# Weight combinations by groups of 128 columns, and three weights decoded in the second part without ScalarE functions

## The chip, the cores and the metric

The kernel runs on one core of a Trainium2 chip. The metric is the time of one execution on the device in microseconds. The engines are named as in the profile: PE (TensorE matmuls), PEld (TensorE weight loads), DVE (VectorE), ACT (ScalarE), POOL (GpSimd), SP (SyncE, which here issues every DMA).

## What is computed

Three layers follow one another on 4 x 3072 tokens of width 256. The float64 weights of the second and third layer arrive as pairs of 32-bit words.

```python
def _attn_ref(x, w_r, w_i, b_r, b_i):              # layer 1: FFT, complex mixing, soft threshold
    X = np.fft.rfft(x, axis=1); Xr, Xi = X.real, X.imag
    Yr = Xr @ w_r - Xi @ w_i + b_r
    Yi = Xr @ w_i + Xi @ w_r + b_i
    Y = soft(Yr, 0.01) + 1j * soft(Yi, 0.01)
    return np.fft.irfft(Y, n=x.shape[1], axis=1)
def _moe_ref(x, w_in, w_out):                      # layer 2: 256 -> 2048 -> 256
    h = x @ w_in
    return (h * np.tanh(softplus(h))) @ w_out
def _moe2_ref(x, mu_k, mu_r, w_k, w_v, w_r):       # layer 3: 256 -> 1024 -> 256, gated
    xk = mu_k * x + (1 - mu_k) * x_prev;  xr = mu_r * x + (1 - mu_r) * x_prev
    k = np.maximum(xk @ w_k, 0)
    return sigmoid(xr @ w_r) * (k * k @ w_v)
```

## The kernel before

**Two parts.** `part1` (L649) does the FFT layer. It runs 48 steps `u`, 12 for each of the four batches. A step emits a forward product F(u+1) (8 matmuls), the mixing product M(u) (13) and the inverse product I(u-1) (8), with the ScalarE and VectorE work that reads their banks: `post_F` (copy `xh`, remainder `xl`), `post_M` and `post_M2` (soft threshold `yb`), `post_I` (copy `bs`, then its store to `b_dr`). Butterflies of the FFT fill DVE in the background: `Background` (L415) keeps a clock of its own, and `bg.until` emits background operations until that clock has reached a time; where a step has weight work to do, 2100 ns are put on that clock (L864, L880). The engines work in the order in which the program emits.

**Float32 by two halves.** A matmul operand is held as a high part (`fp32r`) and a low part (what is left), so that one product is three matmuls: high x high, high x low, low x high.

**Seven products in place of eight.** The first product of layers 2 and 3 multiplies 2 x 2 blocks by seven block products. The four weight blocks and four sums of them are eight fields, of which seven are kept as high and low parts, 14 x 128 columns for each group. `MOVING` (L626) says which combination of the tokens meets which of the seven.

**Decoding the weights.** `raw_piece` (L499) loads 256 x 256 float64 values as words. `decode` (L505) makes float32 of them in stages: on ACT `sg` = sign (Copy with a scale, then Sign) and later Abs of the number; on DVE a xor and shift of the high word, an or with the shifted low word, and `min` times `sg`; then ACT copies the high part and DVE subtracts it. `pair_pieces` (L560) decodes two pieces, makes the four sums over 256 columns, splits and stores two groups. `Weights` (L593) is the pipeline: each `vec()` takes a new piece and advances the three before it, `sca` does the ACT stages and then issues the next loads. In steps 6 to 14 (`PARK_AT`, L41) `w_k` goes through it, 4 pieces, stored to `k_dr`. In the 12 steps of the last batch 8 pieces of `w_in` (stored to `h_dr`) and 8 of `w_out` (kept in SBUF) go through it, two pieces a step (L874 to L880). The first loads are issued in step 35.

**Part 2 by a planner.** `part2` (L909) hands every operation to `Plan` (L97) with an engine, a holding time and a due time. The plan runs the list in modelled time: an engine that is free takes the ready operation with the least due time, however far off that due time is, and this order is what is emitted. There are 12 stretches `J` of 1024 tokens, each 8 groups `n` of layer 2 (planned 10.22 us each, `at(n)`), then 48 groups of layer 3. A group (`group`, L934) is seven products into banks `x`, `c`, `d`, `z` with ACT copies between them (`c<-x`, `d<-x`, `zs<-z`) and two DVE sums (`k<-c`, `k<-d`); `outs_of` (L988) then makes the function of the result (ACT Mish in layer 2), its high and low parts (`h`, `l`) and the second product (`a<-h,wo`). `moving` (L1056) makes the combinations of the tokens, in the order of `MOVING`. `f3_job` (L1083) does the rest of the FFT butterflies on DVE. Weights `wr` of layer 2 are loaded again for each group from `h_dr`.

**The five pieces decoded in part 2** (L1156 to L1187): `w_v` (4 pieces) and the gate's weight, one after the other through one tile `dec`, each with a load, two ACT operations for the sign (`a1` Copy, `a2` Sign), `v1`, `v2` on DVE, `a3` Abs on ACT, `v3` on DVE, `a4` and `v4` for the two parts, and a store. They start behind the last butterfly job, with due times from `at(64)` on and 40 us apart. `dec_done`, the last store, is what the loads of layer 3's weights (`wk`, `wv`, L1212) and of the gate's operand (L1266) wait for.

Of the kernel before, what the change touches and what calls it, by code (L numbers as in the profile page):

```python
# [11 lines left out]
F32 = mybir.dt.float32  # L12
F32R = mybir.dt.float32r
I32 = mybir.dt.int32
# [26 lines left out]
PARK_AT = (6, 15)  # L41
# [127 lines left out]
def tile_fft_mix_moe_channel_mix(  # L169
# [26 lines left out]
    def emit(ops):  # L196
        for e in ops:
            e()

    def tt(o, a, b, op):  # L200
        V.tensor_tensor(out=o, in0=a, in1=b, op=op)  # L201
# [4 lines left out]
    def act(o, i, f, **kw):  # L206
        S.activation(out=o, in_=i, func=f, **kw)  # L207
# [291 lines left out]
    def raw_piece(src):  # L499
        raw = pools["st"].tile([128, 512, 2], I32, tag="raw", name="raw", bufs=4)  # L500
        nc.sync.dma_start(out=raw.rearrange("p (k f) t -> p k (f t)", k=2),
                          in_=src.bitcast(I32).rearrange("(k p) f -> p k f", p=128))
        return raw

    def decode(raw, place, parts):  # L505
        words = raw.rearrange("p (k f) t -> p k f t", k=2)
        hw, lw = words[:, :, :, 1], words[:, :, :, 0]
        tl = {}
        two = lambda z: z.rearrange("p (k f) -> p k f", k=2)
# [40 lines left out]
    def park_piece(w, dst, stage):  # L550
        raw = raw_piece(w)
        tl = {}

        def parts(q):
            t = tl["t"] = stage()
            return [(t[:, 0, :].rearrange("p (k f) -> p k f", k=2), t[:, 1, :].rearrange("p (k f) -> p k f", k=2), q)]
        a0, v0, v1, a2, v2, a1 = decode(raw, flat_q, parts)
        return a0, v0, v1, a2, lambda: v2() + [lambda: nc.sync.dma_start(out=dst, in_=tl["t"].bitcast(F32))], a1

    def pair_pieces(w, dst, i, m, field, stage):  # L560


        f = {}

        def first():
            return decode(raw_piece(w[:, 256 * i:256 * i + 256]),
                          lambda: f.setdefault("s", field())[:, 0:4:3, :], lambda q: [])

        def second():
            a0, v0, v1, a2, v2, a1 = decode(raw_piece(w[:, 256 * (i + m):256 * (i + m) + 256]),  # L570
                                            lambda: f["s"][:, 4:7:2, :], lambda q: [])
            s = lambda k: f["s"][:, k, :]
            part = lambda t, a, b, w: t[:, :, a:b, w, :].rearrange("p g m f -> p m g f")
            pair = lambda a, b: f["s"][:, a:b, :].rearrange("p m (g f) -> p m g f", g=2)

            def sums():
                return v1() + [lambda: tt(s(1), s(4), s(0), SUB), lambda: tt(s(2), s(6), s(1), SUB),
                               lambda: tt(s(5), s(6), s(4), SUB), lambda: tt(s(7), s(3), s(2), SUB)]

            def highs():  # L580
                t = f["t"] = stage()
                return [lambda: act(part(t, 0, 4, 0), pair(0, 4), ACTF.Copy), lambda: act(part(t, 4, 7, 0), pair(5, 8), ACTF.Copy)]

            def lows():
                t = f["t"]
                put = lambda g: nc.sync.dma_start(out=dst[2 * i + g], in_=t[:, g].rearrange("p m s f -> p (m s) f").bitcast(F32))
                return [lambda: tt(part(t, 0, 4, 1), pair(0, 4), part(t, 0, 4, 0).bitcast(F32), SUB),
                        lambda: tt(part(t, 4, 7, 1), pair(5, 8), part(t, 4, 7, 0).bitcast(F32), SUB),
                        lambda: put(0), lambda: put(1)]
            return a0, v0, sums, highs, lows, a1  # L590
        return [first, second]
# [34 lines left out]
    MOVING = [6, 0, 1, 4, 2, 3, 5]  # L626
# [22 lines left out]
    def part1():  # L649
        with ExitStack() as es:  # L650
# [169 lines left out]
            for u in range(NU):  # L820
# [9 lines left out]
                if u == NU - NT - 1:  # L830
                    mv[0] = big.tile([128, 2, 7, 512], F32R, tag="big", name="yc")
                    flat = mv[0].rearrange("p a b f -> p (a b f)")
                    half = [flat[:, 3584 * i:3584 * i + 3584].rearrange("p (g m s f) -> p g m s f", g=2, m=7, s=2) for i in range(2)]
                    wfield = src_p.tile([128, 2, 8, 256], F32, tag="src", name="wsrc")
                    todo = []
                    for i in range(4):
                        todo += pair_pieces(w_in, h_dr, i, 4, lambda i=i: wfield[:, i % 2], lambda i=i: half[i % 2])
                    todo += [lambda i=i: wout_piece(i) for i in (0, 4, 1, 5, 2, 6, 3, 7)]
                    wq = Weights(todo)
                    wq.load(4)  # L840
                dec = 0
                if b == NB - 1:
                    dec = 2
                elif PARK_AT[0] <= u < PARK_AT[1]:
                    dec = 1
                    if u == PARK_AT[0]:
                        wfield = src_p.tile([128, 2, 8, 256], F32, tag="src", name="wsrc")
                        todo = []
                        for i in range(2):
                            todo += pair_pieces(w_k, k_dr, i, 2, lambda i=i: wfield[:, i],  # L850
                                                lambda: g_p.tile([128, 2, 7, 2, 128], F32R, tag="g", name="wst"))
                        wq = Weights(todo)
                        wq.load(2)
# [19 lines left out]
                if dec:  # L873
                    emit(wq.sca(3 if b == NB - 1 else 2))  # L874
                if u > 1:
                    post_I(u - 2)
                if dec == 2:
                    emit(wq.vec())
                    emit(wq.sca(3 if b == NB - 1 else 2))
                    bg.clock += 2100  # L880
# [18 lines left out]
            while wq.busy():  # L899
                emit(wq.vec())  # L900
                emit(wq.sca(3 if b == NB - 1 else 2))
# [7 lines left out]
    def part2():  # L909
        with ExitStack() as es:  # L910
# [23 lines left out]
            def group(n, tiles, need, weights, outs):  # L934
# [39 lines left out]
                m6 = add("PE", 0.68, b + 0.25 * T, product(2, "x", False), need(2), p11)  # L974
                m2 = add("PE", 0.68, b + 0.27 * T, product(3, "p11", False), need(3), p11)
# [10 lines left out]
                return [m1, m5, m6, m2, m7, m3, m4]  # L986
# [170 lines left out]
            prev, due = f3_end, at(64)  # L1157
            sl = lambda a, b: dec["g"][:, a:b]
            two = lambda z: z.rearrange("p (k f) -> p k f", k=2)
            words = lambda j: sl(0, 1024).bitcast(I32).rearrange("p (k f t) -> p k f t", k=2, t=2)[:, :, :, j]  # L1160
            sg, q_ = lambda: two(sl(1024, 1536)), lambda: two(sl(1536, 2048))
            hi_, lo_ = lambda: two(sl(2048, 2560).bitcast(F32R)), lambda: two(sl(2560, 3072).bitcast(F32R))
            for i in range(5):
                src = w_v[256 * i:256 * i + 256, :] if i < 4 else w_g

                def begin(i=i, src=src):
                    if i == 0:
                        dec["g"] = g_p.tile([128, 4096], F32, tag="g", name="dec")
                    nc.sync.dma_start(out=sl(0, 1024).bitcast(I32).rearrange("p (k f) -> p k f", k=2),
                                      in_=src.bitcast(I32).rearrange("(k p) f -> p k f", p=128))  # L1170
                ld = add("SP", 2.6, due, begin, prev, land=8.0)
                a1 = add("ACT", 0.54, due + 6, lambda: act(sg().bitcast(I32), words(1).bitcast(F32), ACTF.Copy, scale=14000.0), ld)
                a2 = add("ACT", 0.54, due + 8, lambda: act(sg(), sg().bitcast(I32), ACTF.Sign), a1)
                v1 = add("DVE", 0.6, due + 6, lambda: V.tensor_scalar(
                    out=q_().bitcast(I32), in0=words(1), scalar1=0x08000000, scalar2=3,
                    op0=ALU.bitwise_xor, op1=ALU.logical_shift_left), ld)
                v2 = add("DVE", 0.6, due + 8, lambda: stt(
                    q_().bitcast(I32), words(0), 29, q_().bitcast(I32), ALU.logical_shift_right, ALU.bitwise_or), v1)
                a3 = add("ACT", 0.54, due + 10, lambda: act(q_(), q_(), ACTF.Abs), v2)
                v3 = add("DVE", 0.6, due + 12, lambda: stt(q_(), q_(), 3.4e38, sg(), ALU.min, MULT), a2, a3)  # L1180
                a4 = add("ACT", 0.54, due + 14, lambda: act(hi_(), q_(), ACTF.Copy), v3)
                v4 = add("DVE", 0.6, due + 16, lambda: tt(lo_(), q_(), hi_().bitcast(F32), SUB), a4)
                st = add("SP", 2.6, due + 17, lambda i=i: nc.sync.dma_start(
                    out=v_dr[i], in_=sl(2048, 3072).rearrange("p (s f) -> p s f", s=2)), v4, land=8.0)
                prev = [st, v4]
                due += 40
# [184 lines left out]
```

## Time and profile before

| | before |
|---|---|
| median of 3 runs | 1897.53 us (1897.16 to 1899.59) |
| profiled execution, its own time | 1898.92 us |
| span of the profiled execution | 1897.1 us |
| PE busy | 1860.3 us, 98% of the span, 9654 matmuls |
| DVE busy | 1412.3 us, 74% |
| ACT busy | 1211.3 us, 64% |
| mean granted clock | 0.998 |

PE is busy nearly all the time, so the time left to gain is in the few stretches where PE waits or runs at a lower clock. The profile counts matmuls as pipelined: a row of PE with x3 is three matmuls, and idle time in brackets is counted from the modelled end of the matmul before.

### The profile page before, as it was taken

To read this page: it belongs to the slowest core of one execution; us is meant where nothing else is said; L and a number is where in the kernel's file an instruction comes from. 1 tells how busy PE (TensorE), PEld (TensorE's weight loads), DVE (VectorE), ACT (ScalarE), POOL (GpSimd) and SP (SyncE) were. 2 spreads that over 40 slices of the span, in tenths; PEclk is the share of its full clock that TensorE was granted. 3 is DMA by queue.
4 is the path that set the end of the run, shared out by engine and by line. 5 is a ranking of instruction groups with operands and counts; after the bars stand their busy time and mean duration, and the time that the engine had idled before them with its cause. 6 is when DMAs were issued, how large, how long until landed. Compare 5 with 4: busy or idle time off the path is not lost.

```text
span 1897.1 us, 26716 instructions
## 1 busy us (share of the span) xinstructions
PE 1860.3 (98%) x9654; PEld 1598.4 (84%) x9654; DVE 1412.3 (74%) x2565; ACT 1211.3 (64%) x2143; POOL 9.1 (0%) x16
## 2 busy tenths in 40 slices
PE   6999999999999999999999999999999999999999
PEld 5888878788888888877777888888999999999998
DVE  8999987689688797875767667565676676766654
ACT  2433267666757567576767667575887777777775
POOL 0000000000100000000000000000000000000000
PEclk9999999999999999999999999999999999999999
DMA  9354285555556556544535344455222222222211
GB/s 291 129 177 144 67 287 204 176 180 167 170 169 192 155 160 188 150 159 131 170 120 164 117 153 122 125 160 168 90 78 68 68 67 68 68 69 75 69 47 34
DMA packets 183427, 255.66 MB, mean 135 GB/s; under 512 B 15608, under 2 KB 105344, under 8 KB 183040
## 3 DMA queue, kind: packets, MB, share of 16 engines
q1 hardware_dynamic: 183296, 253.96, 42.3%
q8 instruction: 77, 1.26, 0.3%
q14 instruction: 54, 0.44, 0.1%
HBM read 177.35 MB, written 76.55 MB: 134 GB/s over the span
## 4 chain that ended last, share of the span: by engine, by line
PE 87%; DVE 6%; ACT 4%; DMA 1%; issue 1%; SPq 0%; DVEq 0%; ACTq 0%
PE a L210 25%; PE x L210 15%; PE v L210 14%; PE c L210 10%; PE d L210 5%; PE z L210 5%; PE yps L210 5%; PE zps L210 3%; PE bps L210 3%; PE xps L210 3%; DVE a L201 2%; ACT L207 1%; ACT k L207 1%; DVE wsrc L204 1%; DVE a L204 1%
## 5 line engine op out<-in xcount | busy, mean ns | idle before, releaser
L201 DVE TENSOR_TENSOR l<-k,h 128x512 fp32r<-128x512 f32 x576 | 392.9, 692 | 328.0 <-ACT h L207 170.5
L210 PE MATMUL a<-h,wo 128*128 128x512 f32 x1536 | 523.0, 390 | 0.0
L210 PEld LDWEIGHTS a<-h,wo 128*128 128x128 f32 x1536 | 289.4, 188 | 60.6
L210 PE MATMUL a<-l,wo 128*128 128x512 f32 x768 | 299.7, 390 | 0.5 <-DVE l L201 0.4
L210 PE MATMUL v<-wv,h 128*128 128x256 f32 x1536 | 274.4, 278 | 0.0
L210 PEld LDWEIGHTS v<-wv,h 128*128 128x128 f32 x1536 | 244.4, 188 | 13.7
L210 PE MATMUL x<-yc,wr 128*128 128x512 f32 x864 | 244.3, 391 | 8.9 <-ACT c L207 8.9
L207 ACT ACTIVATE k<-c 128x512 f32<-128x512 f32 x288 | 172.8, 600 | 109.9 <-PE c L210 98.3
L207 ACT ACTIVATE c<-x 128x512 f32<-128x512 f32 x288 | 169.4, 588 | 98.8 <-PE x L210 82.5
L207 ACT ACTIVATE k<-k 128x512 f32<-128x512 f32 x288 | 177.8, 632 | 66.4 <-DVE k L201 63.9
L210 PE MATMUL v<-wv,l 128*128 128x256 f32 x768 | 213.0, 277 | 0.0
L210 PEld LDWEIGHTS x<-yc,wr 128*128 128x128 f32 x864 | 161.4, 188 | 46.6 <-ACT c L207 12.3
L210 PEld LDWEIGHTS a<-l,wo 128*128 128x128 f32 x768 | 144.7, 188 | 31.4 <-DVE l L201 1.3
L207 ACT ACTIVATE d<-x 128x512 f32<-128x512 f32 x144 | 84.7, 588 | 132.4 <-PE x L210 131.4
L210 PE MATMUL c<-yc,wr 128*128 128x512 f32 x576 | 163.0, 392 | 1.7 <-DVE k L201 1.7
L210 PEld LDWEIGHTS v<-wv,l 128*128 128x128 f32 x768 | 144.4, 188 | 0.0
L207 ACT ACTIVATE h<-k 128x512 fp32r<-128x512 f32 x192 | 118.5, 629 | 30.2 <-DVE k L204 28.3
L201 DVE TENSOR_TENSOR k<-d,zs 128x512 f32<-128x512 f32 x144 | 99.1, 688 | 48.8 <-PE d L210 48.6
L210 PEld LDWEIGHTS c<-yc,wr 128*128 128x128 f32 x576 | 108.4, 189 | 25.2 <-DVE k L201 2.6
L201 DVE TENSOR_TENSOR yc<-src,yc 128x512 fp32r<-128x512 f32 x168 | 112.6, 690 | 16.8 <-ACT yc L207 15.8
L210 PE MATMUL x<-yc,wk 128*128 128x512 f32 x432 | 122.5, 392 | 0.0
L201 DVE TENSOR_TENSOR g<-g 128x128 f32<-128x128 f32 (+3 forms) x272 | 113.5, 440 | 0.9
(102 smaller groups left out, 2806.3 us busy)
## 6 DMA issues: line engine op xcount, KB each, us to landing
wr<-h_dr SPq DMA_DIRECT2D x288, 256.0 KB, 2.7
b_dr<-bs SPq DMA_DIRECT2D x48, 256.0 KB, 2.1
src<-y_dr SPq DMA_DIRECT2D x24, 512.0 KB, 4.2
wr<-h_dr SPq DMA_DIRECT2D x96, 128.0 KB, 2.0
xk_dr<-tm SPq DMA_DIRECT2D x48, 256.0 KB, 2.5
xr_dr<-tm SPq DMA_DIRECT2D x48, 256.0 KB, 3.1
xr<-xr_dr SPq DMA_DIRECT2D x24, 512.0 KB, 3.7
src<-xk_dr SPq DMA_DIRECT2D x24, 512.0 KB, 4.3
```

The costliest lines, as they stand in the source:

```text
L201: V.tensor_tensor(out=o, in0=a, in1=b, op=op)
L204: V.scalar_tensor_tensor(out=o, in0=a, scalar=s, in1=b, op0=op0, op1=op1)
L207: S.activation(out=o, in_=i, func=f, **kw)
L210: T.matmul(out=o, lhsT=l, rhs=r, start=start, stop=stop, **kw)
```

## The change

- `PARK_AT` becomes (6, 13), and in those steps `w_in` groups 0 to 3 are decoded in place of `w_k`. From step 33 on (`LAST_AT`) groups 4 to 7 of `w_in` and then the 8 pieces of `w_out` follow, one piece a step; the second call of `vec` and `sca` in a step is gone.
- `group_piece` takes the place of `pair_pieces` and `park_piece`: one piece is four blocks of 128 columns, which are decoded, summed over 128 columns, split and stored as one group. Its load is two DMAs of rows of 1 KB, in place of one of rows of 2 KB.
- The order of the eight fields changes, so products 2 and 3 of a group change places (`MOVING` and two lines of `group`).
- In part 2 nine pieces are decoded: four groups of `w_k`, then `w_v` and the gate. Due times start at `at(52)`. The sign is now put on by shifts: six DVE operations one behind the other (xor and shift; or with the shifted low word; shift left and right by one; `min`; sign bit by two shifts; or), in `w_k` four sums more. On ACT only the copies of the high part are left, one for a piece of `w_v` or the gate, two for `w_k`.

```diff
-PARK_AT = (6, 15)
+PARK_AT = (6, 13)
+LAST_AT = 33
...
+    SUMS_W = [(1, 4, 0), (3, 6, 1), (5, 6, 4), (7, 2, 3)]
+    def group_piece(w, dst, g, field, stage):
+        raw = pools["st"].tile([128, 512, 2], I32, tag="raw", name="raw", bufs=4)
+        for e in range(2):
+            c0 = 128 * g + e * (w.shape[1] // 2)
+            nc.sync.dma_start(out=raw[:, 256 * e:256 * e + 256, :].rearrange("p (k f) t -> p k (f t)", k=2),
+                              in_=w[:, c0:c0 + 128].bitcast(I32).rearrange("(k p) f -> p k f", p=128))
         tl = {}
 
...
+        def place():
+            tl["f"] = field()
+            return tl["f"][:, 0:8:2, :]
+        a0, v0, v1, a2, v2, a1 = decode(raw, place, lambda q: [], 4)
+        def sums():
+            f = tl["f"]
+            return v1() + [lambda o=o, a=a, b=b: tt(f[:, o, :], f[:, a, :], f[:, b, :], SUB) for o, a, b in SUMS_W]
+        def highs():
+            f, t = tl["f"], tl.setdefault("t", stage())
+            return [lambda: act(t[:, 0:4, 0, :], f[:, 0:4, :], ACTF.Copy), lambda: act(t[:, 4:7, 0, :], f[:, 5:8, :], ACTF.Copy)]
+        def lows():
+            f, t = tl["f"], tl["t"]
+            return [lambda: tt(t[:, 0:4, 1, :], f[:, 0:4, :], t[:, 0:4, 0, :].bitcast(F32), SUB),
+                    lambda: tt(t[:, 4:7, 1, :], f[:, 5:8, :], t[:, 4:7, 0, :].bitcast(F32), SUB),
+                    lambda: nc.sync.dma_start(out=dst[g], in_=t.rearrange("p m s f -> p (m s) f").bitcast(F32))]
+        return a0, v0, sums, highs, lows, a1
...
-    MOVING = [6, 0, 1, 4, 2, 3, 5]
+    MOVING = [6, 0, 4, 1, 2, 3, 5]
...
+                if u == PARK_AT[0]:
+                    wf = src_p.tile([128, 4, 8, 128], F32, tag="src", name="wsrc")
+                    ws = g_p.tile([128, 2, 7, 2, 128], F32R, tag="g", name="wst")
+                    wq = Weights([lambda g=g: group_piece(w_in, h_dr, g, lambda g=g: wf[:, g % 4], lambda g=g: ws[:, g % 2])
+                                  for g in range(4)])
+                    wq.load(2)
+                if u == LAST_AT:
+                    wf = src_p.tile([128, 4, 8, 128], F32, tag="src", name="wsrc")
+
+                    def stage(g):
+                        if g == 4:
+                            mv[0] = big.tile([128, 2, 7, 512], F32R, tag="big", name="yc")
+                        flat = mv[0].rearrange("p a b f -> p (a b f)")
+                        return flat[:, 1792 * (g % 4):1792 * (g % 4) + 1792].rearrange("p (m s f) -> p m s f", m=7, s=2)
+                    wq = Weights([lambda g=g: group_piece(w_in, h_dr, g, lambda g=g: wf[:, g % 4], lambda g=g: stage(g))
+                                  for g in range(4, 8)] + [lambda i=i: wout_piece(i) for i in (0, 4, 1, 5, 2, 6, 3, 7)])
+                    wq.load(3)
+                dec = 1 if PARK_AT[0] <= u < PARK_AT[1] or u >= LAST_AT else 0
...
-                if dec == 2:
-                    emit(wq.vec())
-                    emit(wq.sca(3 if b == NB - 1 else 2))
-                    bg.clock += 2100
...
-                m6 = add("PE", 0.68, b + 0.25 * T, product(2, "x", False), need(2), p11)
-                m2 = add("PE", 0.68, b + 0.27 * T, product(3, "p11", False), need(3), p11)
+                m6 = add("PE", 0.68, b + 0.25 * T, product(3, "x", False), need(3), p11)
+                m2 = add("PE", 0.68, b + 0.27 * T, product(2, "p11", False), need(2), p11)
...
-            prev, due = f3_end, at(64)
+            prev, due = f3_end, at(52)
...
+                last = add("SP", 2.6, due, begin, prev, land=8.0)
+                ops = [lambda qi=qi, wd=wd: scalars(qi(), wd(1), 0x08000000, ALU.bitwise_xor, 3, SHL),
+                       lambda qi=qi, wd=wd: stt(qi(), wd(0), 29, qi(), SHR, ALU.bitwise_or),
+                       lambda qi=qi: scalars(qi(), qi(), 1, SHL, 1, SHR),
+                       lambda q_=q_: V.tensor_scalar_min(out=q_(), in0=q_(), scalar1=3.4e38),
+                       lambda si=si, wd=wd: scalars(si(), wd(1), 31, SHR, 31, SHL),
+                       lambda qi=qi, si=si: tt(qi(), qi(), si(), ALU.bitwise_or)]
+                if pair:
+                    ops += [lambda o=o, a=a, b=b: tt(field()[:, o, :], field()[:, a, :], field()[:, b, :], SUB) for o, a, b in SUMS_W]
+                for e, op in enumerate(ops):
+                    last = add("DVE", 0.6 if e < 6 else 0.2, due + 6 + e, op, last)
+                if pair:
+                    views = [lambda k: (ws()[:, 0:4, k, :], field()[:, 0:4, :]), lambda k: (ws()[:, 4:7, k, :], field()[:, 5:8, :])]
+                    dst, area = k_dr[i], lambda: ws().rearrange("p m s f -> p (m s) f")
+                else:
+                    views = [lambda k: (sl(2048 + 512 * k, 2560 + 512 * k), sl(1024, 1536))]
+                    dst, area = v_dr[i], lambda: sl(2048, 3072).rearrange("p (s f) -> p s f", s=2)
+                his = [add("ACT", 0.54, due + 16, lambda v=v: act(v(0)[0].bitcast(F32R), v(0)[1], ACTF.Copy), last) for v in views]
+                los = [add("DVE", 0.6, due + 17, lambda v=v: tt(v(1)[0].bitcast(F32R), v(1)[1], v(0)[0], SUB), h)
+                       for v, h in zip(views, his)]
+                st = add("SP", 4.5 if pair else 2.6, due + 18, lambda dst=dst, area=area: nc.sync.dma_start(out=dst, in_=area()),
+                         los, land=8.0)
+                prev = [st] + los
```

## Rows read from the trace of the kernel before

**Rows 1.** Busy time by stretch: start:end, length, PE, PEld, DVE, ACT, POOL (instructions), clock, DMA

```profile
420.00:820.00 400.00, 400.00 (x1766) 331.22 (x1766) 338.44 (x665) 251.66 (x445) 7.52 (x5) 1.00 0.55 167
840.00:1040.00 200.00, 190.31 (x816) 154.28 (x815) 130.87 (x225) 141.78 (x236) 0.83 (x3) 0.98 0.46 148
1040.00:1240.00 200.00, 200.00 (x884) 165.57 (x883) 127.97 (x220) 124.27 (x220) 0.29 (x2) 1.00 0.42 128
```

**Rows 2.** Whom PE waited for: us in total, times, longest

```profile
PE x L210 <- ACT c L207: 8.9, 7, 2.0
PE bps L210 <- DVE yb L204: 4.2, 4, 1.4
PE c L210 <- DVE k L201: 1.7, 2, 0.9
```

**Rows 3.** All table loads of ACT: count, busy us and mean ns, idle before

```profile
L207 ACT ACT_TABLE_LOAD x17 | 21.8, 1283 | 9.2 <-DMA braw<-in_b_r_dram 9.0
```

**Rows 4.** ACT in order of time, first and second piece: start, us, operation

```profile
837.43 1.28 ACT L207 ACT_TABLE_LOAD   x1
838.73 1.15 ACT L207 ACTIVATE dec<-dec 128x512 f32<-128x512 int32 x2
839.90 1.28 ACT L207 ACT_TABLE_LOAD   x1
...
887.79 1.28 ACT L207 ACT_TABLE_LOAD   x1
889.08 0.63 ACT L207 ACTIVATE dec<-dec 128x512 f32<-128x512 f32 x1
```

**Rows 5.** PE in order of time, at the first of the waits

```profile
842.82 0.39 PE L210 MATMUL a<-h,wo 128*128 128x512 f32 x1
845.24 0.97 PE L210 MATMUL x<-yc,wr 128*128 128x512 f32 x3 [2.02 <-ACT c L207]
```

**Rows 6.** Busy time by stretch, two stretches at a lower clock (columns of Rows 1)

```profile
932.00:936.00 4.00, 4.00 (x11) 3.13 (x12) 2.67 (x5) 2.55 (x5) 0.00 (x0) 0.57 0.14 25
1021.00:1025.00 4.00, 4.00 (x12) 3.10 (x12) 2.02 (x4) 1.69 (x4) 0.00 (x0) 0.57 0.39 123
```

**Rows 7.** PE in order of time: forward products that begin four FFT steps

```profile
225.28 1.89 PE L210 MATMUL xps<-fm,a 128*128 128x256 f32 x8
...
238.10 1.89 PE L210 MATMUL xps<-fm,a 128*128 128x256 f32 x8
...
263.11 1.89 PE L210 MATMUL xps<-fm,a 128*128 128x256 f32 x8
...
319.29 1.89 PE L210 MATMUL xps<-fm,a 128*128 128x256 f32 x8
```

**Rows 8.** DVE in order of time, in the FFT steps

```profile
232.76 2.40 DVE L201 TENSOR_TENSOR g<-g 128x128 f32<-128x128 f32 x7
...
278.18 0.42 DVE L519 TENSOR_SCALAR wsrc<-raw 128x512 int32<-128x512 int32 x1
278.63 0.69 DVE L204 SCALAR_TENSOR_TENSOR wsrc<-raw,wsrc 128x512 int32<-128x512 int32 x1
279.24 2.09 DVE L201 TENSOR_TENSOR yc<-wsrc,yc 128x1024 fp32r<-128x1024 f32 x2
```

**Rows 9.** DVE in order of time: first decode operation of step 6, with its wait

```profile
60.78 0.43 DVE L519 TENSOR_SCALAR wsrc<-raw 128x512 int32<-128x512 int32 x1 [1.84 <-DMA raw<-in_moe_w_k_dram]
```

**Rows 10.** DMA issues by the page: count, KB each, median us from issue to landing

```profile
k_dr<-wst SPq DMA_DIRECT2D x4, 896.0 KB, 5.9
```

**Rows 11.** Decode in part 2: issues of the first two loads and of the last store

```profile
811.78 0.38 SPq L1169 DMA_DIRECT2D dec<-in_moe_w_v_dram  x1
...
870.43 0.44 SPq L1169 DMA_DIRECT2D dec<-in_moe_w_v_dram  x1
...
1033.97 0.38 SPq L1183 DMA_DIRECT2D v_dr<-dec  x1
```

**Rows 12.** PE in order of time: first product of layer 3

```profile
1325.10 0.86 PE L210 MATMUL x<-yc,wk 128*128 128x512 f32 x3
```

More of the change, by code (lines that the diff above doesn't have):

```diff
@@ L503, in raw_piece, with decode @@
         return raw
-    def decode(raw, place, parts):
-        words = raw.rearrange("p (k f) t -> p k f t", k=2)
+    def decode(raw, place, parts, k=2):
+        words = raw.rearrange("p (k f) t -> p k f t", k=k)
         hw, lw = words[:, :, :, 1], words[:, :, :, 0]
         tl = {}
-        two = lambda z: z.rearrange("p (k f) -> p k f", k=2)
+        two = lambda z: z.rearrange("p (k f) -> p k f", k=k)
         def a0():
@@ L548, in wout_piece @@
         return decode(raw, flat_q, parts)
-    def park_piece(w, dst, stage):
-        raw = raw_piece(w)
-        tl = {}
[L554 to L591, printed above, removed]
@@ L829, in part1 @@
                 bg.step()
[L830 to L853, printed above, removed]
+                if u == PARK_AT[0]:
[4 more added lines that the diff above has]
+                    wq.load(2)
@@ L873, in part1 @@
                 if dec:
-                    emit(wq.sca(3 if b == NB - 1 else 2))
+                    emit(wq.sca(3))
                 if u > 1:
                     post_I(u - 2)
-                if dec == 2:
-                    emit(wq.vec())
-                    emit(wq.sca(3 if b == NB - 1 else 2))
-                    bg.clock += 2100
                 emit_M(u)
@@ L900, in part1 @@
                 emit(wq.vec())
-                emit(wq.sca(3 if b == NB - 1 else 2))
+                emit(wq.sca(3))
             post_M(NU - 1)
@@ L985, in group @@
                 plan.after(p21, [first])
-                return [m1, m5, m6, m2, m7, m3, m4]
+                return [m1, m5, m2, m6, m7, m3, m4]
             def outs_of(second, off, f32_of, unit_of, cost):
@@ L1156, in part2 @@
             dec = {}
-            prev, due = f3_end, at(64)
+            prev, due = f3_end, at(52)
             sl = lambda a, b: dec["g"][:, a:b]
[L1159 to L1167, printed above, removed]
-                        dec["g"] = g_p.tile([128, 4096], F32, tag="g", name="dec")
[L1169 to L1185, printed above, removed]
@@ new lines, in part2, with scalars, begin @@
+            words = lambda j: sl(0, 1024).bitcast(I32).rearrange("p (f t) -> p f t", t=2)[:, :, j]
+            sg = lambda: sl(3328, 3840)
+            def scalars(o, i, c1, o1, c2, o2):
+                V.tensor_scalar(out=o, in0=i, scalar1=c1, scalar2=c2, op0=o1, op1=o2)
+            SHL, SHR = ALU.logical_shift_left, ALU.logical_shift_right
+            for kind, i in [("k", g) for g in range(4)] + [("v", i) for i in range(5)]:
+                pair = kind == "k"
+                src = (w_v[256 * i:256 * i + 256, :] if i < 4 else w_g).bitcast(I32)
+                def begin(i=i, src=src, pair=pair):
+                    if not dec:
+                        dec["g"] = g_p.tile([128, 4096], F32, tag="g", name="dec")
+                    raw = sl(0, 1024).bitcast(I32)
+                    if pair:
+                        for e in range(2):
+                            c0 = 128 * i + 512 * e
+                            nc.sync.dma_start(out=raw[:, 512 * e:512 * e + 512].rearrange("p (k f) -> p k f", k=2),
+                                              in_=w_k[:, c0:c0 + 128].bitcast(I32).rearrange("(k p) f -> p k f", p=128))
+                    else:
+                        nc.sync.dma_start(out=raw.rearrange("p (k f) -> p k f", k=2), in_=src.rearrange("(k p) f -> p k f", p=128))
+                field = lambda: sl(1024, 2048).rearrange("p (m f) -> p m f", m=8)
+                ws = lambda: sl(2048, 3840).rearrange("p (m s f) -> p m s f", m=7, s=2)
+                if pair:
+                    q_ = lambda: field()[:, 0:8:2, :]
+                    like = lambda z: z.rearrange("p (m f) -> p m f", m=4)
+                else:
+                    q_ = lambda: sl(1024, 1536)
+                    like = lambda z: z
+                qi = lambda q_=q_: q_().bitcast(I32)
+                si = lambda like=like: like(sg()).bitcast(I32)
+                wd = (lambda j: words(j).rearrange("p (m f) -> p m f", m=4)) if pair else words
+                last = add("SP", 2.6, due, begin, prev, land=8.0)
[5 more added lines that the diff above has]
+                       lambda qi=qi, si=si: tt(qi(), qi(), si(), ALU.bitwise_or)]
+                if pair:
+                    ops += [lambda o=o, a=a, b=b: tt(field()[:, o, :], field()[:, a, :], field()[:, b, :], SUB) for o, a, b in SUMS_W]
+                for e, op in enumerate(ops):
+                    last = add("DVE", 0.6 if e < 6 else 0.2, due + 6 + e, op, last)
+                if pair:
+                    views = [lambda k: (ws()[:, 0:4, k, :], field()[:, 0:4, :]), lambda k: (ws()[:, 4:7, k, :], field()[:, 5:8, :])]
+                    dst, area = k_dr[i], lambda: ws().rearrange("p m s f -> p (m s) f")
+                else:
+                    views = [lambda k: (sl(2048 + 512 * k, 2560 + 512 * k), sl(1024, 1536))]
[6 more added lines that the diff above has]
+                prev = [st] + los
```

## The prediction

> **What bounds the kernel now.** I read the busy times first, then the stretches, then whom PE waited for, then the engines in order of time around each wait. PE is idle for 37 us of the 1897.1 us of the span: at the start, where it waits for the first tokens, and at the tail, both unchanged, and mostly in two places that the change touches. In the stretch from 420 to 820 us PE is busy 400.00 of 400 us, with DVE at 338.44, 85%; from 1040 to 1240 it is busy 200.00 of 200 [rows 1]. Between them, from 840 to 1040 us, it is idle 9.69 us and carries 816 matmul records where the next 200 us carry 884 [rows 1]. Those 200 us are where the five pieces are decoded in part 2 [rows 11]. The waits there are for ACT's copy `c<-x` and, less often, for DVE's `k` [rows 2]. The other place is the last batch of the FFT, where PE waits for DVE's `yb` [rows 2].
>
> **Part 2: the table loads go.** Within one piece ACT loads a table before Sign and Abs (837.43) and another to return to Mish (839.90); each takes 1.28 us and the next operation follows 0.01 to 0.02 us later [rows 4]. Fourteen of the 17 table loads [rows 3] lie in this decode: two each in three of the pieces, four each in the two pieces in which other work came between Sign and Abs, as at 887.79, where Abs alone is preceded by one [rows 4]. PE's copy `c<-x` stands behind them in ACT's order. At the first wait PE goes from a start at 842.82 to the next at 845.24, 2.42 us, where matmuls follow each other every 400/1766 = 0.23 us [rows 1, 5]. So a wait costs 2.42 - 0.23 = 2.19 us, 0.17 us more than the 2.02 us written at it [rows 5], since idle time is counted from a modelled end. Seven waits lie in the stretch, so 9.69 + 7 x 0.17 = 10.9 us.
>
> After two of the five stalls the granted clock fell to its lower level of 1.2 GHz for a while: its mean over 4 us is 0.57 at 932 and again at 1021 us, after full clock until the stall [rows 6]. That loses 2 x 4 x (1 - 0.57) = 3.4 us. No other stretch that I looked at is below full clock, so I take it to come with the stalls. Sum: 10.9 + 3.4 = 14.3 us. The count of matmuls says the same in another way: (884 - 816) / 884 x 200 = 15.4 us [rows 1]. I keep 14.3.
>
> The change takes Sign and Abs, with the scaled Copy ahead of them, off ACT in part 2, 15 operations. What is left there is Copy, which ACT runs between Mish operations all through layer 2 without a load: only 3 of 17 loads lie outside the decode [rows 3]. So I expect all 14 to go, and the whole 14.3 us. The Trainium skill, "ScalarE: Activation LUTs", section "Table sets: the hidden batching unit", lists abs among the functions that every set has; the load ahead of Abs alone disagrees, and Copy agrees. Its section "What ACT_TABLE_LOAD costs" gives about 2.66 us for a switch with its drain; by that a pair would hold ACT 5.3 us, and five pairs at PE would make 27 us in place of 10.9. The trace decides, and the sum uses it.
>
> **Part 2: what comes in its place on DVE.** By spacings in the trace, a 512-wide scalar operation takes 0.45 us, one with two tensors 0.61, and a 128-wide one 2.40/7 = 0.34 [rows 8]. A piece of `w_v` or the gate then takes four scalar operations at 0.45 and three at 0.61, 3.6 us (before: 0.45 + 3 x 0.61 = 2.3). The `min` alone has no row of its own; its ends are 0.45 and 0.61, and I take 0.45, the same form. A group of `w_k` takes 4 x 0.45 + 2 x 0.61 + 4 x 0.34 and two low parts of together about 1.1, so 5.5 us. In all 4 x 5.5 + 5 x 3.6 - 5 x 2.3 = 28.5 us more on DVE, over some 400 us. DVE is at 131/200 = 65% there and would be at 73%; at 85% PE was never idle [rows 1]. I cost it at 0.5 us; the bounds are nothing, and one wait like `c<-k` (0.86 + 0.17 us, [rows 2]) for each of nine pieces, 9.3 us. If the cover of the other DVE work's slack were gone, it is `k<-c` and `k<-d` that would be late next, and PE's product in bank `c`.
>
> The first operation behind a load moves from ACT and DVE to DVE alone. Behind it on DVE stand `k`, `l` and the sums of the tokens. Loads were always there in time before: no DMA is among whom PE waited for [rows 2], and the plan gives a load 10.6 us. SP gets 8 loads of `w_k`, 4 stores of 896 KB and the nine pieces' waits in its order; the `wr` loads queued behind are planned 1.8 groups, 18 us, ahead, against 5.9 us for such a store [rows 10]. Nothing for that. The exchange of products 2 and 3 moves no work; nothing.
>
> **Part 1: one piece a step.** A step without decode takes (238.10 - 225.28)/2 = 6.41 us. From 263.11 to 319.29 us eight steps take 56.18, which is 56.18 - 8 x 6.41 = 4.9 us too long [rows 7]. Two pieces of `w_in` cost DVE, in such a step, 2 x (0.45 + 0.61 + 0.61) for decode, four sums 256 wide (between 0.34 and 0.61 each), 2.0 for two low parts, and 1.2 for `yb` and `xl`: 7.9 to 9.0 us, over 6.41 [rows 8]. In the new kernel a step holds one piece: 0.45 + 0.61 + 0.61 + 4 x 0.34 + 1.1 + 1.2 = 5.3 us, below 6.41, so PE should set each step again: all 4.9 us return. ACT has one piece too. The Trainium skill, "VectorE: DVE Perf Modes", section on the TRN2 errata, speaks against groups of 128: a fixed cost for each instruction, so tile to 512 or more. The row agrees (0.34 for 128, not a quarter of 0.61), and even so the step fits.
>
> Against it: step 33 issues its loads and decodes in the same step, behind butterflies that still run. The same pattern stands in step 6, where DVE waited 1.84 us for the load and PE lost nothing [rows 9]. From DVE's timeline some 9 us of butterflies are left at step 33; with 2.1 us a step set aside they last to step 36, when low parts of the first group join. I cost this at 0.5 us, between nothing and two waits as long as the longest for `yb`, 2 x 1.4 [rows 2]. In steps 6 to 12 the staging area has two halves, so ACT's high parts of group g+2 wait for the store of g: 5.9 us [rows 10] against a step of 6.41. That is covered, by little; uncovered it delays `bs` on ACT, of which PE needs nothing for a step. Nothing.
>
> **The sum.** From the profiled execution's own 1898.92 us (span 1897.1 and 1.8 around it): 1898.9 - 10.9 - 3.4 - 4.9 + 0.5 + 0.5 = 1880.7. The median of the runs is 1.4 us below the profiled one, so 1879.3 by that; I say **1880.0**.
>
> **The rivals.** (1) *DVE takes ACT's place.* Six to ten DVE operations in a row for each of nine pieces delay `k`, and PE waits as it did for `c<-k`. For it: DVE is what PE waits for in two of three rows of waits [rows 2]. Against it: 85% of DVE with no idle PE [rows 1]. Price 9.3 us in full: 1889. (2) *Part 1 returns nothing.* Steps 33 to 38 lose as much to DVE as the old double steps: 4.4 more than I take, 1885. For it: DVE is still the fullest engine there. Against it: 5.3 against 6.41 us. (3) *Slower: the decode ends too late.* `dec_done` now comes after nine pieces that share one tile and run one behind the other. Before, five took 1033.97 - 811.78 = 222 us, 44.4 each, the first 58.7 [rows 11]. Nine at 44.4, from some 807 us, end at 1207; the first product of layer 3 will stand at about 1325 - 19 = 1306 [rows 12]. At 54.5 us a piece and more, allowing some 8 us for store and load, PE waits at the start of layer 3; at 58.7 the decode ends at 1335, and some 37 us are lost: 1917. Against it: the due times come 40 us apart, from earlier on, so late pieces go ahead of other work. (4) *The table loads stay,* since Copy to this tile would need one: only part 1's gain is left, 1893, at the edge of no change.
>
> **Chances.** Forecast 0.65 (1877 to 1884), (1) 0.15, (2) 0.10, (3) 0.06, (4) 0.04. About 0.2%, 3.8 us, is what a measurement of this kernel can tell from no change. Half of (4) counts as the same, with 0.01 for mixtures. Faster 0.91, same 0.03, slower 0.06. The range is 1877 to 1890: below, as 15.4 in place of 14.3 and nothing lost anew would give 1877; above, it takes in (1) and (2) and leaves out (3) and (4).
>
> **What would show it.** Right: three table loads in all, PE busy 200 of 200 us from 820 to 1020 with about 884 records, clock 1.00 there, FFT steps of 6.41 us from step 33 to 47, no new row among whom PE waited for. Wrong: a row PE from DVE `k` grown to several microseconds (1); steps over 6.41 at 33 to 38 with waits for `yb` (2); the last decode store after some 1290 us and PE waiting for a DMA at layer 3's start (3); table loads next to `dec` (4).

## The result: faster by 0.8%, all of it from part 2

| | before | after |
|---|---|---|
| median | 1898.56 us (4 runs) | 1882.89 us (1880.64 to 1884.37, 4 runs) |
| ratio, 95% interval | | 0.9916 (0.9899 to 0.9933) |
| profiled execution, its own time | 1898.92 us | 1884.37 us |
| span | 1897.1 us | 1882.6 us |
| PE busy | 1860.3 us | 1855.6 us |
| ACT table loads | 17 | 3 |

The median lies 2.9 us above the predicted 1880.0 us, inside the range of 1877 to 1890. The two profiled executions differ by 14.5 us of span, and four marks in PE's order of time say where. At the forward product that starts at 238.10 us in [rows 7] the changed kernel is 1.64 us later; of that, 0.82 us are there already at the first product, where PE waits for the first tokens. This start is spread and not the change: the changed kernel run again began 0.50 us earlier. At the first product of layer 2 the changed kernel is 1.00 us later, at the first product of layer 3 it is 14.33 us earlier (1325.10 in [rows 12]), and the rest gives 0.17 us more. The first view is of the kernel before, the second of the changed one:

```profile
332.58 0.85 PE L210 MATMUL x<-yc,wr 128*128 128x512 f32 x3
```

```profile
239.74 1.89 PE L211 MATMUL xps<-fm,a 128*128 128x256 f32 x8
...
333.58 0.85 PE L211 MATMUL x<-yc,wr 128*128 128x512 f32 x3
...
1310.77 0.86 PE L211 MATMUL x<-yc,wk 128*128 128x512 f32 x3
```

So part 1 gave back nothing on balance, and part 2 gave 1.00 + 14.33 = 15.3 us.

In part 2, the stretch of [rows 1] in the changed kernel (stretch, length, PE, PEld, DVE, ACT, POOL, clock, DMA), and all its table loads:

```profile
840.00:1040.00 200.00, 200.00 (x884) 165.56 (x883) 148.10 (x277) 126.80 (x226) 0.37 (x2) 1.00 0.53 167
```

```profile
L208 ACT ACT_TABLE_LOAD x3 | 3.8, 1283 | 9.1 <-DMA braw<-in_b_r_dram 9.0
```

PE is busy 200.00 of 200 us with 884 matmul records, in place of 190.31 and 816, and the clock is 1.00 all through. Fourteen table loads [rows 3] are gone. DVE has 148 us of work in place of 131.

Whom PE waited for in the changed kernel (us in total, times, longest), against [rows 2]:

```profile
PE bps L211 <- DVE yb L205: 2.8, 3, 2.0
PE x L211 <- ACT c L208: 1.2, 2, 0.7
```

The wait for `c<-x` falls from 8.9 to 1.2 us, and the row for DVE's `k` is gone. The wait for `yb` stays: of the 4.2 us before, 3.9 lay in the double steps and went, while 2.00 us came at one place, step 36, and 0.62 us in step 9. The rest, 0.16 us in step 12, was there before too (0.25). Step 36 in the changed kernel:

```profile
252.04 1.89 PE L211 MATMUL xps<-fm,a 128*128 128x256 f32 x8
259.04 3.57 PE L211 MATMUL bps<-im,yb 128*128 128x256 f32 x8 [2.00 <-DVE yb L205]
262.40 2.04 PE L211 MATMUL xps<-fm,a 128*128 128x256 f32 x8
```

From 252.04 to 262.40 the step takes 10.36 us. The same step of the kernel before, with the long mixing product of a batch's first step, took 6.57. Of the 3.8 us lost, 2.0 are the wait and most of the rest is clock, 4 x (1 - 0.57) = 1.7 us in the four microseconds behind it:

```profile
259.00:263.00 4.00, 3.96 (x11) 3.20 (x12) 3.90 (x10) 1.63 (x4) 0.00 (x0) 0.57 0.99 332
```

What led there is read from DVE and ACT in order of time:

```profile
235.07 0.43 DVE L520 TENSOR_SCALAR wsrc<-raw 128x512 int32<-128x512 int32 x1 [2.62 <-DMA raw<-in_moe_w_in_dram]
...
251.27 0.68 DVE L202 TENSOR_TENSOR xl<-xps,xh 128x512 fp32r<-128x512 f32 x1
253.41 1.16 DVE L202 TENSOR_TENSOR yc<-wsrc,yc 128x512 fp32r<-128x512 f32 x2 [1.45 <-ACT yc L208]
255.57 0.69 DVE L205 SCALAR_TENSOR_TENSOR wsrc<-wsrc,sg 128x512 f32<-128x512 f32 x1 [1.00 <-ACT wsrc L208]
```

```profile
251.99 0.63 ACT L694 ACTIVATE zl<-xl 128x512 fp32r<-128x512 f32 x1 [3.24 <-DVE xl L202]
```

DVE waits 2.62 us for the first load of step 33 and then runs late through three steps of butterflies and decode. For the first product of a batch, and only there, ACT copies `zl` from DVE's `xl`. ACT stands still for 3.24 us before it, and its decode operations behind it come late. DVE then waits for those, 1.45 and 1.00 us, with `yb` queued behind. The two engines hand one delay back and forth.

### The profile page after: what moved, and what is told of

Same layout as the page of the kernel before. It is cut to its first block, busy times and chain, and to the rows that moved or that the text cites. A ratio compares the mean times of both kernels' runs of the same rounds, so it can differ in the third digit from the quotient of the medians.

```text
span 1882.6 us, 26775 instructions
## 1 busy us (share of the span) xinstructions
PE 1855.6 (99%) x9654; PEld 1597.8 (85%) x9654; DVE 1420.5 (75%) x2628; ACT 1179.2 (63%) x2114; POOL 8.9 (0%) x16
## 4 chain that ended last, share of the span: by engine, by line
PE 92%; DVE 6%; DMA 1%; ACT 1%; SPq 0%; issue 0%; DVEq 0%
PE a L211 27%; PE x L211 16%; PE v L211 14%; PE c L211 10%; PE d L211 5%; PE z L211 5%; PE yps L211 5%; PE zps L211 4%; PE bps L211 3%; PE xps L211 3%; DVE a L202 2%; DVE a L205 1%; DVE wsrc L205 1%; DVE yb L205 1%; DVE xl L202 0%; DMA raw<-in_moe_w_in_dram 0%
```

## Experiments

Two theories for step 36: W, the load that DVE waits for in step 33; R, too little time set aside for the decode on the butterflies' clock. Two for part 2: T, the table loads were the whole loss; M, a good part comes from what else was moved. And for DVE in part 2: S, it has room; D, the longer chains delay the sums `k`. The first four kernels ran side by side (before: 1899.38 us), and then the next four (before: 1899.44 us).

**The changed kernel again**, as the reference for the three runs that follow.

> The changed kernel as it is, as the reference for the three runs beside it. Both theories: 0.990 to 0.993 of the kernel before; at step 36 PE waits about 2 us for DVE's yb, since DVE waited some 2.6 us for the load in step 33.

1881.34 us (1880.53 to 1881.96), ratio 0.9906 (0.989 to 0.9923). DVE's wait in step 33 was 1.68 us here, PE's wait 1.34, with no fall of the clock behind it:

```profile
257.67 2.00 PE L211 MATMUL bps<-im,yb 128*128 128x256 f32 x8 [1.34 <-DVE yb L205]
```

So the loss at step 36 is not one number: 3.8 us in the first profile, 1.6 us (8.17 in place of 6.57) in this one. A longer wait for the load and half clock behind the stall make the difference, and with it part of the spread between executions: of the four runs of the result, the two slower ones (1884.37 and 1883.79 us) have a mean clock of 0.999 and the two faster ones (1880.64 and 1881.99 us) of 1.000.

**Loads of the last stretch one step earlier.**

```diff
-                if u == LAST_AT:
+                if u == LAST_AT - 1:
```

> The changed kernel with the loads of the last decode stretch issued one step earlier (step 32 in place of 33), nothing else. Theory W (DVE falls behind because it waits for the first load in step 33): DVE's wait of 2.6 us goes, PE's wait at step 36 falls from 2.0 us to under 0.5, the FFT steps from 33 on are 6.41 us again, and the span is 3 to 4.5 us shorter than the changed kernel's. Theory R (2.1 us set aside a step are too few for the decode, so butterflies crowd DVE): the wait at step 36 stays above 1 us, and the span is less than 1.5 us shorter.

1879.72 us, ratio 0.9898 (0.9883 to 0.9913): 1.6 us less than the changed kernel beside it. DVE's wait for a load is gone, and step 36 takes what it took before (250.77 to 257.33 us, 6.56):

```profile
250.77 1.89 PE L211 MATMUL xps<-fm,a 128*128 128x256 f32 x8
257.33 1.89 PE L211 MATMUL xps<-fm,a 128*128 128x256 f32 x8
```

W's mechanism holds; its size of 3 to 4.5 us did not, since the stall it was read from was the larger one.

**More time set aside.**

```diff
-                    bg.clock += 2100
+                    bg.clock += 2100 if u < LAST_AT else 3600
```

> The changed kernel with 3600 ns in place of 2100 set aside on the butterflies' clock for each decode step from 33 on, loads as they are. Theory W: DVE still waits 2.6 us in step 33, and PE's wait at step 36 falls by less than half. Theory R: the wait at step 36 goes, 3 to 4.5 us shorter than the changed kernel. The four butterflies per step that are put off run in steps 36 to 40, where DVE has room.

1879.93 us, 0.9899 (0.9884 to 0.9914). DVE still waits 1.81 us in step 33, but PE's wait in step 36 is 0.22 us: R works too, though not to the last: step 36 takes 7.05 us, 0.5 more than with the early loads. The long stall needs both, a late start and a full queue behind it, and either one taken away removes most of it.

```profile
256.31 2.00 PE L211 MATMUL bps<-im,yb 128*128 128x256 f32 x8 [0.22 <-DVE yb L205]
```

**Both.**

> Both edits: loads one step earlier and 3600 ns set aside. Theory W: as with the loads alone, within 0.5 us. Theory R: as with the clock alone. If each holds half of the cause: shorter than either by 1 us or more, about 4.5 us shorter than the changed kernel, 0.989 of the kernel before.

1879.83 us, 0.9899 (0.9884 to 0.9913): no better than either, so the cause has no two halves that add. The small wait of step 36 is there again (0.20 us, the step takes 7.03), as with the clock alone, though DVE waits for no load in step 33 here.

**Shifts alone, in the kernel before.** The five pieces of part 2 get the DVE chain; part 1 and the due times stay.

```diff
-                a1 = add("ACT", 0.54, due + 6, lambda: act(sg().bitcast(I32), words(1).bitcast(F32), ACTF.Copy, scale=14000.0), ld)
-                a2 = add("ACT", 0.54, due + 8, lambda: act(sg(), sg().bitcast(I32), ACTF.Sign), a1)
...
-                a3 = add("ACT", 0.54, due + 10, lambda: act(q_(), q_(), ACTF.Abs), v2)
-                v3 = add("DVE", 0.6, due + 12, lambda: stt(q_(), q_(), 3.4e38, sg(), ALU.min, MULT), a2, a3)
...
+                        lambda: scalars(qi(), qi(), 1, SHL, 1, SHR),
+                        lambda: V.tensor_scalar_min(out=q_(), in0=q_(), scalar1=3.4e38),
+                        lambda: scalars(si(), words(1), 31, SHR, 31, SHL),
+                        lambda: tt(qi(), qi(), si(), ALU.bitwise_or)]):
+                    v3 = add("DVE", 0.6, due + 6 + e, op, v3)
```

> The kernel before with one part of the change alone: the sign of the five pieces in part 2 put on by shifts on DVE (six operations one behind the other), so that ACT keeps only the copy of the high part. Part 1 and the due times stay. Theory T (the table loads were the whole loss in part 2): 3 table loads, PE 200.00 of 200 us from 840 to 1040 with about 884 records, 14.3 to 15.4 us shorter than the kernel before, 0.992. Rival M (a good part of the gain comes from moving w_k, the earlier due times or part 1): less than 8 us shorter.

1883.69 us, ratio 0.9917 (0.9902 to 0.9932), 15.8 us less. PE is busy 200.00 of 200 us, and there are 3 table loads, while the waits for `yb` are still 4.2 us in 4 times, three of them in the double steps:

```profile
840.00:1040.00 200.00, 200.00 (x883) 165.56 (x883) 142.24 (x252) 125.39 (x222) 0.38 (x2) 1.00 0.52 159
```

T holds and M falls: this one part gives all that part 2 gave. From the first product of layer 2 to the first of layer 3 it is 992.52 us before, 977.19 in the changed kernel and 977.03 (333.64 to 1310.67) here. Against the 1881.34 us of the whole change in the set of runs before, with nearly the same time of the kernel before, all the other edits together are worth some 2.3 us.

**Sign and Abs put back on ACT, for all nine pieces.**

```diff
-                       lambda qi=qi: scalars(qi(), qi(), 1, SHL, 1, SHR),
...
-                       lambda qi=qi, si=si: tt(qi(), qi(), si(), ALU.bitwise_or)]
+                a1 = add("ACT", 0.54, due + 6, lambda si=si, wd=wd: act(si(), wd(1).bitcast(F32), ACTF.Copy, scale=14000.0), last)
+                a2 = add("ACT", 0.54, due + 8, lambda si=si, sf=sf: act(sf(), si(), ACTF.Sign), a1)
...
+                a3 = add("ACT", 0.54, due + 10, lambda q_=q_: act(q_(), q_(), ACTF.Abs), v2)
```

> The changed kernel with the sign of all nine pieces in part 2 put back on ACT (scaled Copy, Sign, Abs) and the four DVE operations less that this saves. Theory T: at least 18 more table loads, about 2.2 us of waits for each piece and 0.7 us of half clock on average, 9 x 2.9 = 26 us (20 without the clock) longer than the changed kernel, so slower than the kernel before. Rival M: within 8 us of the changed kernel.

1912.22 us, ratio 1.0064 (1.0049 to 1.0079): slower than before, and 30.9 us over the changed kernel. Not all of that is the table loads: in the profiled execution step 36 takes 10.01 us, against 8.17 in the changed kernel run again. Part 2, between the same two products as above, takes 1005.33 us, 28.2 more than the 977.17 there, or 3.1 for each piece. T again, a little dearer than the 26 us expected: 26 loads came in nine pieces, and the longest single wait was 3.7 us.

```profile
PE x L211 <- ACT c L208: 17.9, 10, 3.7
PE c L211 <- DVE k L202: 2.8, 2, 1.9
```

```profile
L208 ACT ACT_TABLE_LOAD x29 | 37.2, 1283 | 9.9 <-DMA braw<-in_b_r_dram 9.4
```

So moving `w_k` into part 2 without the shifts would have lost more than part 1 could give. The row for DVE's `k` also comes and goes with the table loads: it was never DVE's own load.

**Twelve more DVE operations in each piece.**

```diff
+                ops = ops[:6] + [lambda qi=qi, si=si: tt(si(), qi(), si(), ALU.bitwise_or)] * 12 + ops[6:]
```

> The changed kernel with twelve more DVE operations of 512 columns in the chain of each of the nine pieces in part 2 (they write a scratch area): 9 x 12 x 0.61 = 66 us more DVE work. Theory S (DVE has room, so its share of the decode is free): within 1.5 us of the changed kernel, PE 200 of 200 us from 840 to 1040, decode ending later. Rival D (DVE operations delay the sums k that PE needs): if one piece's six operations cost up to 1 us, eighteen cost 3 us, so 10 us or more longer, with waits of PE for DVE k.

1881.78 us, 0.9908 (0.9893 to 0.9923), 0.4 us over the changed kernel of the set before, within the spread of the runs. From 800 to 1150 us DVE is busy 292 of 350 us, 83%, and PE 350.00 with no wait:

```profile
800.00:1150.00 350.00, 350.00 (x1546) 289.76 (x1545) 292.21 (x536) 224.31 (x400) 1.14 (x4) 1.00 0.50 153
```

S holds, D falls. The last store of the decode starts at 1241.6 us here. Layer 3 still begins on time, 977.02 us behind the first product of layer 2, but from there to the end it takes 572.35 us in place of the 571.79 of the changed kernel run again, with a wait of 0.43 us for ACT's `r` at 1351.79 us; what brought that wait is not shown.

**First loads of both stretches one step earlier.**

```diff
-                if u == PARK_AT[0]:
+                if u == PARK_AT[0] - 1:
...
-                if u == LAST_AT:
+                if u == LAST_AT - 1:
```

> The changed kernel with the first loads of both decode stretches issued one step earlier (steps 5 and 32). Theory W: DVE waits for no load in step 6 either, PE's wait for yb in step 10 (0.4 to 1.0 us in the four profiles so far) goes, and the time is 0.5 to 1 us below the run with the second stretch's loads alone early, 0.989 of the kernel before. Rival: the wait in step 10 comes from butterflies that are due there and stays.

1878.08 us (1877.77 to 1878.60), ratio 0.9887 (0.9871 to 0.9904), the fastest of all kernels here: 3.3 us under the changed kernel and 1.6 under the run with only the second stretch's loads early, each set against nearly the same time of the kernel before. That is more than the 0.5 to 1 us expected. The row for `yb` is gone altogether:

```profile
PE xps L211 <- DVE g L202: 18.0, 2, 16.6
PE x L211 <- ACT c L208: 1.2, 2, 0.7
PE yps L211 <- ACT zl L695: 0.3, 1, 0.3
PE a L211 <- DVE l L202: 0.2, 1, 0.2
```

So the wait that the expectation puts in step 10 (0.62 us in the changed kernel's first profile) came from the load of step 6 too. Counted as in step 36, it stands in step 9, between the forward products at 79.37 and 86.67 us:

```profile
84.83 1.99 PE L211 MATMUL bps<-im,yb 128*128 128x256 f32 x8 [0.62 <-DVE yb L205]
```

Step 12, the beginning of the second batch, gained as well: it takes 6.57 us here, against 7.01 with only the second stretch's loads early and 7.08 in the kernel before. Against the shifts alone this kernel is 5.6 us faster, all of it in part 1: from the first forward product to the first product of layer 2 it takes 311.09 us in place of 316.72. So the 4.9 us that the prediction hoped for in part 1 were there, and the 0.5 of step 12 with them.

## Why the prediction was right, and where it was not

- **Bounds, and the table loads in part 2: right.** The cause, its place and the disappearance of all 14 loads came as written, and the shifts alone showed that nothing else in the change is needed for it.
- **Its size: 14.3 us was 1.0 low; 15.3 was measured.** The second count, 15.4 from the missing matmul records, was right. The term that was short is the stall's own price: 2.19 us counts to the start of the first matmul behind it, but the three behind a stall take 0.97 us [rows 5], where three in a row take 0.84 elsewhere (at 848.11 us, for one), so seven stalls hold about 7 x 0.13 = 0.9 us more. Nothing contradicts the clock's 3.4 us.
- **DVE's added work in part 2 at 0.5 us: right, and it cost nothing.** PE never waits for `k`, and with twelve more operations in each chain part 2 is no longer than without them.
- **The decode's end: the fear was too large.** The last store starts at 1149.5 us, (1149.5 - 812.8)/9 = 37.4 us a piece, below the 44.4 that rival (3) started from. ACT's stages were part of what made the pieces slow: the shifts alone, with the old due times, bring the five pieces to (1019.5 - 812.9)/5 = 41.3 us, and with Sign and Abs back on ACT the nine take (1167.7 - 812.4)/9 = 39.5. The earlier due times remain as the reason for the rest, and no run tried them alone.
- **One piece a step: right.** From step 38 on the steps take 6.41 us, and the eight steps that took 56.18 us take 51.31, from 268.99 to 320.30. The 4.9 us came back, and the losses in steps 36 and 9 ate them.
- **Step 33 at 0.5 us: wrong.** It cost 4.25 us in the first profile (0.31 in the step before step 36, 3.79 in it, 0.15 behind), 1.6 us in the second. The step that failed is the reading of the precedent: in step 6 PE lost nothing in the next steps to a wait of 1.84 us, so step 33 was taken as harmless, and the bound of 2 x 1.4 us was no bound. Two things differ. The changed kernel makes the four sums in every step, the kernel before in every second, so DVE has less room to catch up: from the first decode operation of step 6 to `yb` of step 9 it works without a gap in both kernels, 22.9 us in the changed one (61.21 to 84.10) and 20.2 before (60.78 to 81.01). And behind step 33 a batch begins three steps later, where ACT waits for DVE. The clock behind a stall, counted in part 2, was not counted here.
- **A nearer precedent was overlooked.** In the kernel before, the loads of the double steps are issued in step 35, and DVE waits 4.24 us for the first of them in step 36; PE's waits for `yb` [rows 2] follow in steps 38 to 40. So the 4.9 us that the prediction put down to two pieces a step stand behind a late load too. How much of them an earlier load alone would have given back, no run here shows. The line, of the kernel before:

```profile
251.17 0.43 DVE L519 TENSOR_SCALAR wsrc<-raw 128x512 int32<-128x512 int32 x1 [4.24 <-DMA raw<-in_moe_w_in_dram]
```

- **Steps 6 to 12 at nothing: wrong** by 0.9 and 0.65 us in the first two profiles, at step 9. No batch begins there, and DVE waits for nothing between the load and the late `yb`: the late start alone is enough for a small loss. With both loads early the loss is gone and the staging area is as it was, so the staging had no part in it.
- So the sign that was set for rival (2), steps over 6.41 us at 33 to 38 with a wait for `yb`, came in the profiled execution, beside the forecast of part 2; in later runs, at about half its price. That the median came within 2.9 us of 1880.0 is in part luck: part 2 gave 1.0 us more than was counted, against a loss of 2 to 5 us in part 1. The range held because it had been drawn to take rival (2) in.

## What to carry to other kernels

An operation that needs another table costs the two loads around it, on the queue where they stand; where a tight chain passes through that queue, look for a form on another engine, even at twice the operations there, if that engine was elsewhere fuller without harm. When a load is issued in the same step as its first reader, try it one step earlier: here that cost nothing but a buffer that was already there, and gave 3.3 us in two places together. A precedent for a harmless wait holds only if the steps behind it are alike: add up what the engine that starts late has to do in them, and look for the next place at which two engines wait for each other.

## What was not expected of the hardware

- A single Abs between Mish operations had a table load before it [rows 4] and another behind it, at 891.12 us, while a Copy at 882.13 had none before it. Both lines are of the kernel before:

```profile
882.13 0.66 ACT L207 ACTIVATE dec<-dec 128x512 int32<-128x512 f32 x1
...
891.12 1.28 ACT L207 ACT_TABLE_LOAD   x1
```

- A wait of PE of about 2.0 us left the clock alone in one case (at 845 us, before) and was followed by some 4 us around half clock in others (before: two [rows 6]; after: step 36). Waits of 1.34 and 1.61 us in step 36 of other runs were not followed by it, nor were 1.90 and 1.95 us in part 2 with Sign and Abs back on ACT, where 3.38 and twice 3.68 us were. What decides between the cases near 2 us stays open.
